# One weight tile on a second DMA queue in the opening of a SwiGLU kernel, with one warm-up matmul fewer

## Chip, cores and metric

The kernel runs on one core of one Trainium2 chip. The metric is the device time of one execution in microseconds (us). Engines are named PE (matmul), PEld (weight load, overlaps PE), ACT (ScalarE), DVE (VectorE), POOL (GpSimd) and SP (SyncE). SP and ACT can both issue DMAs; the notes below call these "SP's queue" and "ACT's queue". The profile's span is about 1.8 us shorter than the measured time, and all times inside a profile count from the span's start.

## The reference

All values are bf16; x is 1 x 2048 x 512, w_gate and w_up are 512 x 1376, w_down is 1376 x 512.

```python
def reference(x, w_gate, w_up, w_down):
    g = silu(x @ w_gate)
    u = x @ w_up
    return (g * u) @ w_down
```

## The kernel before

x is loaded in four chunks of 512 rows, each transposed by the DMA on its way, so that the contracted dimension (512, four blocks `dk` of 128) lies on the partitions. Weights come in growing column blocks. Until the first x chunk and the first gate tile have landed, PE multiplies a constant ("dummies"), so that it is not idle and its clock is let up to full rate.

```python
N_WARM = 11
...
        o = load_x("sp", 0)                      # 512 rows x 512 columns, 512 KB, transposed
        for dk in range(KD):
            got_x[0, dk] = o
        for a, b in ((0, 1), (1, 2), (2, 4), (4, 7), (7, NFT)):
            g = load_w("sp", w_gate, 0, a * P, min(b * P, F))
            u = load_w("sp", w_up, UPH, a * P, min(b * P, F - 32))
            for ft in range(a, b):
                for dk in range(KD):
                    got_g[ft, dk], got_u[ft, dk] = g, u
        ...
        op("act", lambda e: e.activation(adummy[:, 0:4], zero_c, ACT.Silu), inc=False)

        for i in range(N_WARM):
            op("pe", lambda e: e.matmul(banks[7][:, :], lhsT=ones_w, rhs=ones_m, start=True, stop=True), inc=False)
        ...
        def mm_g(n, c, ft, dk):
            deps = [got_x[c, dk], got_g[ft, dk]]
            ...
```

The first real matmul therefore waits for two loads: the whole first x chunk (one transposing DMA) and the first gate tile (128 KB). Everything after it, four chunks of gate and up matmuls with silu on ACT and the product on DVE and then the down projection, is one dense stream on PE.

## Time and profile before

| | before |
|---|---|
| time, median of 3 runs (lowest to highest) | 123.04 us (122.6 to 123.08) |
| span of the profiled run | 121.0 us |
| PE busy | 117.1 us, 97% |
| x chunk issued, landed | 0.73, 4.80 us |
| first gate tile issued, landed | 2.18, 5.45 us |
| first real matmul | 5.59 us |

The page of the kernel before says in its first part which engine is busy, and in its fourth part (the chain of work that ended last) that this work is nearly all on PE.

```profile
PE 117.1 (97%) x540; PEld 53.3 (44%) x550; DVE 43.8 (36%) x64; ACT 30.2 (25%) x51; POOL 0.2 (0%) x4
PE 97%; issue 1%; ACT 0%
```

So, without touching the matmuls, only the two ends can be shortened: the opening, and the 2.5 us from the last matmul's end (about 118.6 us) to the end of the span. The timeline of SP in the opening, kernel before (start, duration, then the instruction; "SPq" is the issue of a DMA, not its transfer):

```profile
0.73 1.39 SPq L123 DMA_TRANSPOSE xT_sb<-in_x_dram  x1
2.18 0.57 SPq L131 DMA_DIRECT2D w_sb<-in_w_gate_dram  x1
2.81 0.48 SPq L131 DMA_DIRECT2D w_sb<-in_w_up_dram  x1
```

The DMA view of the first microseconds, kernel before (size and time from issue to landing):

```profile
w_sb<-in_w_gate_dram SPq DMA_DIRECT2D x1, 128.0 KB, 3.3
xT_sb<-in_x_dram SPq DMA_TRANSPOSE x1, 4.1
```

The gate tile waits 1.45 us for its turn to be issued and lands 0.65 us after x. PE and its weight loads in the opening, kernel before (the bracket is the idle time before, and what ended it):

```profile
0.77 4.85 PE L163 MATMUL bank<-const-bfloat16-1.0 128*128 128x512 bf16 x11 [0.77 <-PEq L302]
5.59 10.76 PE L166 MATMUL bank<-xT_sb,w_sb 128*128 128x512 bf16 x47
4.14 0.15 PEld L163 LDWEIGHTS bank<-const-bfloat16-1.0 128*128 128x128 bf16 x1 [0.28 <-issue]
4.57 0.15 PEld L163 LDWEIGHTS bank<-const-bfloat16-1.0 128*128 128x128 bf16 x1 [0.27 <-issue]
5.56 0.14 PEld L166 LDWEIGHTS bank<-xT_sb,w_sb 128*128 128x128 bf16 x2 [0.84 <-DMA xT_sb<-in_x_dram]
```

Weight loads start 0.43 us apart: PE runs at half rate here (later matmuls start 0.216 us apart). The last line blames x for the wait, but x had landed at 4.80 us; the gate tile, at 5.45 us, is the load whose landing lies just before 5.56 us. A wait for several semaphores has one name in the profile, and it is worth checking against the landings.

### The profile page before, as it was taken

To read this page: it belongs to the slowest core of one execution; us is meant where nothing else is said; L and a number is where in the kernel's file an instruction comes from. 1 tells how busy PE (TensorE), PEld (TensorE's weight loads), DVE (VectorE), ACT (ScalarE), POOL (GpSimd) and SP (SyncE) were. 2 spreads that over 40 slices of the span, in tenths; PEclk is the share of its full clock that TensorE was granted. 3 is DMA by queue.
4 is the path that set the end of the run, shared out by engine and by line. 5 is a ranking of instruction groups with operands and counts; after the bars stand their busy time and mean duration, and the time that the engine had idled before them with its cause. 6 is when DMAs were issued, how large, how long until landed. Compare 5 with 4: busy or idle time off the path is not lost.

```text
span 121.0 us, 1373 instructions
## 1 busy us (share of the span) xinstructions
PE 117.1 (97%) x540; PEld 53.3 (44%) x550; DVE 43.8 (36%) x64; ACT 30.2 (25%) x51; POOL 0.2 (0%) x4
## 2 busy tenths in 40 slices
PE   7999999999999999999999999999999999999991
PEld 2244444444444444444444444344444444444470
DVE  0024334444334444334354334467242233224230
ACT  4032333262333272333262333230000000000001
POOL 0000000000000000000000000000000000000000
PEclk9999999999999999999999999999999999999999
DMA  3999999900000000000000000000211211121121
GB/s 72 245 285 372 262 236 239 355 29 0 0 0 0 0 0 5 0 0 3 0 3 0 0 0 0 5 0 0 87 43 43 87 43 46 51 81 43 43 73 57
DMA packets 17990, 8.51 MB, mean 70 GB/s; under 512 B 11360, under 2 KB 17984, under 8 KB 17984
## 3 DMA queue, kind: packets, MB, share of 16 engines
q1 hardware_dynamic: 17840, 8.36, 25.3%
q8 instruction: 4, 0.07, 0.2%
q10 hardware_dynamic: 144, 0.07, 0.2%
q14 instruction: 2, 0.02, 0.0%
HBM read 4.23 MB, written 2.10 MB: 52 GB/s over the span
## 4 chain that ended last, share of the span: by engine, by line
PE 97%; issue 1%; ACT 0%
PE bank L166 60%; PE bank L247 31%; PE bank L163 4%; PE bank L221 2%; ACT o_sb L254 0%
## 5 line engine op out<-in xcount | busy, mean ns | idle before, releaser
L166 PE MATMUL bank<-xT_sb,w_sb 128*128 128x512 bf16 x330 | 72.6, 380 | 0.3
L166 PEld LDWEIGHTS bank<-xT_sb,w_sb 128*128 128x128 bf16 x336 | 32.9, 98 | 40.4 <-DMA xT_sb<-in_x_dram 0.8
L188 DVE TENSOR_TENSOR hT_sb<-sg_sb,bank 128x512 bf16<-128x512 f32 x40 | 27.5, 688 | 45.3 <-PE bank L166 45.2
L247 PE MATMUL bank<-wd_sb,hT_sb 128*128 128x512 bf16 (+3 forms) x183 | 37.9, 366 | 0.3 <-issue 0.2
L185 ACT ACTIVATE sg_sb<-bank 128x512 f32<-128x512 f32 x40 | 23.8, 596 | 44.6 <-PE bank L166 44.6
L247 PEld LDWEIGHTS bank<-wd_sb,hT_sb 128*128 128x128 bf16 (+1 forms) x187 | 18.2, 98 | 20.2 <-issue 0.4
L255 DVE CAST o_sb<-bank 128x512 bf16<-128x512 f32 (+1 forms) x16 | 10.8, 675 | 23.7 <-PE bank L247 23.7
L254 ACT ACTIVATE o_sb<-bank 128x256 bf16<-128x256 f32 x1 | 0.4, 384 | 38.9 <-PE bank L247 38.9
L163 PE MATMUL bank<-const-bfloat16-1.0 128*128 128x512 bf16 x11 | 4.9, 630 | 0.8 <-PEq L302 0.8
L212 DVE TENSOR_TENSOR hT_sb<-sgx_sb,bank 32x512 bf16<-32x512 f32 x4 | 2.8, 693 | 4.9 <-ACT sgy_sb L210 4.9
L209 ACT ACTIVATE sgx_sb<-bank 32x512 f32<-32x512 f32 x4 | 2.4, 588 | 4.5 <-PE bank L166 4.5
L163 PEld LDWEIGHTS bank<-const-bfloat16-1.0 128*128 128x128 bf16 x11 | 1.5, 143 | 3.2 <-issue 3.2
L227 DVE TENSOR_TENSOR hT_sb<-sgy_sb,bank 64x512 bf16<-64x512 f32 x4 | 2.7, 684 | 0.1
L210 ACT ACTIVATE sgy_sb<-bank 64x512 f32<-64x512 f32 x4 | 2.4, 589 | 0.1
L221 PE MATMUL bank<-xT_sb,w_sb 128*64 128x512 bf16 x16 | 1.9, 382 | 0.0
L159 ACT ACT_TABLE_LOAD x1 | 1.3, 1283 | 0.7 <-PEq L302 0.7
L221 PEld LDWEIGHTS bank<-xT_sb,w_sb 128*64 128x64 bf16 x16 | 0.8, 109 | 1.0 <-issue 0.4
L159 ACT ACTIVATE act_dummy<-const-float32-0.0 128x4 f32<-128x4 f32 x1 | 0.2, 205 | 0.0
L302 POOL MEMSET const-bfloat16-1.0<- 128x1 bf16 x1 | 0.1, 101 | 0.0
L302 POOL MEMSET const-uint8-127<- 128x1 uint8 x1 | 0.1, 101 | 0.0
L302 POOL MEMSET const-float32-0.0<- 128x1 f32 x1 | 0.1, 98 | 0.2 <-issue 0.2
L302 POOL MEMSET const-float32-1.0<- 128x1 f32 x1 | 0.1, 98 | 0.0
## 6 DMA issues: line engine op xcount, KB each, us to landing
out_dram<-o_sb SPq DMA_DIRECT2D x15, 128.0 KB, 1.7
wd_sb<-in_w_down_dram SPq DMA_DIRECT2D x1, 1280.0 KB, 6.8
w_sb<-in_w_gate_dram SPq DMA_DIRECT2D x1, 480.0 KB, 6.0
w_sb<-in_w_up_dram SPq DMA_DIRECT2D x1, 448.0 KB, 6.5
w_sb<-in_w_gate_dram SPq DMA_DIRECT2D x1, 384.0 KB, 5.0
w_sb<-in_w_up_dram SPq DMA_DIRECT2D x1, 384.0 KB, 5.5
w_sb<-in_w_gate_dram SPq DMA_DIRECT2D x2, 128.0 KB, 3.1
w_sb<-in_w_up_dram SPq DMA_DIRECT2D x2, 128.0 KB, 3.3
```

Source lines behind the costliest of these rows:

```text
L159: op("act", lambda e: e.activation(adummy[:, 0:4], zero_c, ACT.Silu), inc=False)
L163: op("pe", lambda e: e.matmul(banks[7][:, :], lhsT=ones_w, rhs=ones_m, start=True, stop=True), inc=False)
L166: return op("pe", lambda e: e.matmul(bank[:, :], lhsT=w_sb[:, dk, col0:col0 + P], rhs=xT_sb[:, dk, c * SC:(c + 1) * SC], start=(dk == 0), ...
L185: s = op("act", lambda e: e.activation(sg_sb[n % NSG][:, :], psG[n % NG][:, :], ACT.Silu), [g, mults[n - NSG] if n >= NSG else None])
L188: mults.append(op("dve", lambda e: e.tensor_tensor(hT_sb[:, ft, c * SC:(c + 1) * SC], sg_sb[n % NSG][:, :], psU[n % NU][:, :], ALU.mult), ...
L209: op("act", lambda e, c=c: e.activation(sgx_sb[c][96:128, :], psX[64:96, :], ACT.Silu), [xm], inc=False)
L210: rest_a[c] = op("act", lambda e, c=c, y0=y0, y1=y1: e.activation(sgy_sb[c][y0:y1, :], psX[0:64, :], ACT.Silu), [xm])
L212: rest_x[c] = op("dve", lambda e, c=c: e.tensor_tensor(hT_sb[64:96, NFF, c * SC:(c + 1) * SC], sgx_sb[c][96:128, :], psX[96:128, :], ALU.m ...
L221: ym = op("pe", lambda e, pi=pi, dk=dk, c=c, y0=y0, y1=y1: e.matmul(psY[pi][y0:y1, :], lhsT=w_sb[:, dk, YC0:YC0 + 64], rhs=xT_sb[:, dk, c ...
L227: rest_y[c] = op("dve", lambda e, pi=pi, c=c, y0=y0, y1=y1: e.tensor_tensor(hT_sb[0:64, NFF, c * SC:(c + 1) * SC], sgy_sb[c][y0:y1, :], ps ...
L247: om = op("pe", lambda e, K=K, fk=fk: e.matmul(bank[:, 0:ncol], lhsT=hT_sb[0:K, fk, t * P:(t + 1) * P], rhs=wd_sb[0:K, fk, c0:c0 + ncol], ...
L255: return op("dve", lambda e: e.tensor_copy(ob[:, a:b], bank[:, a - c0:b - c0]), deps)
```

## The change

The intent: load the first gate tile from ACT's queue, beside the long issue of the x transpose, so that it no longer waits its turn on SP; with x alone left to wait for, one dummy fewer fits.

```diff
-N_WARM = 11
+N_WARM = 10
...
-        HF = 0
         o = load_x("sp", 0)
...
-            g = load_w("sp", w_gate, 0, a * P, min(b * P, F))
+            g = load_w("act" if a == 0 else "sp", w_gate, 0, a * P, min(b * P, F))
```

(`HF` was not used.)

## The prediction

> **What bounds the kernel now.** TensorE. On the page of the kernel before, PE is busy 117.1 us of a span of 121.0 us; the chain of work that ended last is PE for 97%. After the first real matmul no load or eviction holds PE up, so only a shorter opening can help here.
>
> **The opening, from the timeline and the landing times of the loads.** The eleven dummies start at 0.77 us, 0.427 us apart, so the slot after the eleventh is at about 5.42 us. SP issues the x transpose at 0.73 us for 1.39 us; it lands at 4.80 us. The first gate tile is issued at 2.18 us and lands at 5.45 us, the first up tile at 5.90 us. The first real matmul starts at 5.59 us, 0.14 us after the gate tile: that tile ended the wait (the waits view names x, 0.8 us, before that weight load). The first two real matmuls are still slow; from 6.26 us on, starts are 0.216 us apart, so full rate came at about 6.1 us.
>
> **What the change does.** The gate tile is issued from ACT at about 0.73 us, beside the transpose issue. The issue should take about 0.55 us and pushes the 1.28 us activation table load back; the first real activation is at 6.9 us, so this costs nothing. The gate's 128 KB can be moved before the first x packet (2.1 us). Every later SP issue comes about 0.6 us earlier; the up tile takes the gate's old place and should land near 5.4 us, needed at about 6.4 us. Then x alone releases PE: 4.80 + 0.14 = 4.94 us. Ten dummies end at 0.77 + 10 x 0.427 = about 5.0 us. The first real matmul moves from 5.59 to about 5.0 us: 0.59 us.
>
> **How much reaches the end.** Not all. The Trainium skill, "TensorE: Matmul & The Clock Gate", Part 1, says a free-running activity window, not a count of matmuls, sets the release to full rate; this trace agrees in the two spacings, 0.427 and 0.216 us. PE is busy either way, so the release stays near 6.1 us and the 0.59 us are won at half rate: worth about 0.3 us. In runs where it comes before 5.0 us, all 0.59 us are won. Mean about 0.35 us, 0.3%. Later weight tiles land 0.6 us or more ahead of use and move earlier too.
>
> **Prediction: 122.55 us, 122.0 to 123.05 in 8 of 10.** Faster by over 2%: 0.01; within 2%: 0.98; slower by over 2%: 0.01.
>
> **What would show each step right or wrong.**
> - DMA issues: the gate issue on ACT starts near 0.73 us and lands well before 4 us; x lands at 4.7 to 5.0 us.
> - Timeline: first real matmul at 4.95 to 5.1 us, three real matmuls at slow spacing instead of two; full rate from about 6.1 us.
> - Waits: PE waits at most 0.2 us for x, and for no later weights.
> - Span about 120.7 us.
>
> **What would make it wrong.** The Trainium skill, "Perfetto Trace Analysis", section "DMA Instruction — HWDGE", says the descriptor generator is shared and locked. No trace here shows two queues issuing at once. If ACT gets it first, the transpose is delayed by up to about 0.5 us, x lands near 5.3 us and PE waits after the tenth dummy: the gain falls to about 0.1 us. If ACT must wait, gate packets interleave with x's and delay x as much. A gap in PE could also put the full-rate release off by a window: up to 1.5 us slower. The spread of runs before (122.6 to 123.08 us) is as large as the expected gain.

## The result, and the profile after

| | before | after |
|---|---|---|
| time, median of 4 runs | 122.9 us (122.6 to 123.08) | 122.22 us (122.13 to 122.28) |
| span of the profiled run | 121.0 us | 120.4 us |
| gate tile issued, landed | 2.18 (SP), 5.45 us | 0.74 (ACT), 3.14 us |
| x chunk issued, landed | 0.73, 4.80 us | 0.73, 5.14 us |
| first real matmul | 5.59 us | 5.18 us |
| full rate reached | 6.1 us | about 3.5 us |

The ratio was 0.9947, 95% interval 0.9923 to 0.9971: within 2%. A ratio here is the mean time of one kernel's fast runs over that of the other's fast runs of the same rounds, so not quite the ratio of the medians quoted.

The issues in the opening, kernel after, from the timelines of SP and ACT:

```profile
0.73 1.41 SPq L123 DMA_TRANSPOSE xT_sb<-in_x_dram  x1
0.74 0.42 ACTq L131 DMA_DIRECT2D w_sb<-in_w_gate_dram  x1
1.19 1.28 ACT L158 ACT_TABLE_LOAD   x1 [1.19 <-PEq L301]
```

The two issues run side by side, and the transpose's is not lengthened: 1.41 us beside ACT's, 1.39 us alone. The same loads in the DMA view, kernel after:

```profile
w_sb<-in_w_gate_dram ACTq DMA_DIRECT2D x1, 128.0 KB, 2.4
xT_sb<-in_x_dram SPq DMA_TRANSPOSE x1, 4.4
```

The gate tile is early now, but x takes 0.3 us longer to land. PE and PEld in the opening, kernel after:

```profile
0.77 3.65 PE L162 MATMUL bank<-const-bfloat16-1.0 128*128 128x512 bf16 x10 [0.77 <-PEq L301]
5.18 2.12 PE L165 MATMUL bank<-xT_sb,w_sb 128*128 128x512 bf16 x9 [0.77 <-DMA xT_sb<-in_x_dram]
2.86 0.15 PEld L162 LDWEIGHTS bank<-const-bfloat16-1.0 128*128 128x128 bf16 x1 [0.28 <-issue]
3.28 0.15 PEld L162 LDWEIGHTS bank<-const-bfloat16-1.0 128*128 128x128 bf16 x1 [0.28 <-issue]
3.60 0.32 PEld L162 LDWEIGHTS bank<-const-bfloat16-1.0 128*128 128x128 bf16 x2 [0.16 <-issue]
```

Two things are to be seen. PE now truly waits for x, 0.77 us, because its dummies ran out early. And they ran out early because full rate came between 3.28 and 3.60 us: the step between two loads falls from 0.43 to 0.32 us and then two of them fit in 0.32 us. In the kernel before, the dummies ran at half rate to their end. Up to that moment PE did exactly the same in both kernels, so this difference needs another reason than the change. The two spans differ by 0.65 us, of which 0.40 us is the earlier first real matmul (5.59 to 5.18 us) and about 0.25 us is the two matmuls that before still ran at half rate.

So there are two questions. Does the moment of full rate belong to the change or to chance? And why does x land later, so that the start moved by 0.40 us and not by the 0.59 us of the prediction?

### The profile page after: what moved, and what is told of

It reads as the page before. It is cut to its first block, busy times and chain, and to the rows that moved or that the text cites. A ratio compares the mean times of both kernels' runs of the same rounds, so it can differ in the third digit from the quotient of the medians.

```text
span 120.4 us, 1381 instructions
## 1 busy us (share of the span) xinstructions
PE 116.4 (97%) x549; PEld 53.0 (44%) x549; DVE 43.8 (36%) x64; ACT 30.2 (25%) x51; POOL 0.2 (0%) x4
## 4 chain that ended last, share of the span: by engine, by line
PE 94%; DMA 4%; ACT 0%; issue 0%
PE bank L165 60%; PE bank L246 32%; DMA xT_sb<-in_x_dram 4%; PE bank L220 2%; ACT o_sb L253 0%
## 5 line engine op out<-in xcount | busy, mean ns | idle before, releaser
L162 PE MATMUL bank<-const-bfloat16-1.0 128*128 128x512 bf16 x10 | 3.6, 538 | 0.8 <-PEq L301 0.8
```

## The experiments

Twelve kernels ran, all with correct results. Each comparison with before uses runs of before on the same chip, in rounds.

**Theory.** (1) The moment of release to full rate is chance, in a range of about one window (the free-running window of the clock that the prediction names). (2) x lands later because the gate tile's packets use the same DMA engines just before and while x's first packets want to leave. **Rivals.** The release belongs to the kernel; the dummy that was dropped won the time; the later x is noise; the later x is a fixed cost of a second queue that issues at the same moment, whatever its bytes.

### Each kernel again, and each half of the change alone

The kernel before against itself (no edit):

> The kernel before, once more, against itself: ratio 1.000 within 0.3%. It tells what repeats. Theory: the x transpose lands at 4.8 us and the gate tile at 5.4 to 5.5 us in every trace, first real matmul near 5.6 us. Rival, the landing times are noise: x lands anywhere from 4.7 to 5.2 us, as in the kernel after. The moment of the release to full rate (6.1 us in the first trace of before, 3.4 us in that of after) should fall anywhere between about 3 and 6.5 us if it is a free-running window; if it belongs to the kernel, it comes at 6.1 us again.

The changed kernel again (no edit):

> The changed kernel once more. Ratio to before 0.993 to 0.998. Theory: x lands at 5.1 us again (0.34 us later than alone), gate at about 3.1 us, first real matmul near 5.2 us; the start alone is worth 0.40 us (0.3%), and the rest of the 0.65 us between the two first traces was the chance of the release, 0.25 us. If the release belongs to the kernel it comes at 3.4 us again; if it is free-running it may come anywhere from 3 to 6.5 us, and when after 5.2 us it costs half of the difference.

The gate tile on ACT, eleven dummies:

```diff
-N_WARM = 10
+N_WARM = 11
```

> The gate tile on ACT alone, eleven dummies kept. Theory: x lands at 5.1 us. Where the release comes early, the eleven dummies end before that and the start is the same 5.2 us as with ten; where it comes late they end at 5.42 us and the first real matmul is at 5.42 us, but at the slow rate a dummy more costs little. So ratio to before 0.995 to 0.999, at most 0.2% slower than with ten. Rival, dropping the dummy is what won the time: ratio 1.000.

Ten dummies, the gate tile on SP:

```diff
-N_WARM = 11
+N_WARM = 10
```

> Ten dummies alone, the gate tile kept on SP. Theory: the gate tile at 5.45 us holds the first real matmul at 5.6 us as before, ratio 1.000 within 0.2%; only the idle time before it grows (by up to 0.43 us). Rival, the dummy's time was won: ratio 0.996.

| kernel | median us | ratio to before (95%) | x landed | gate landed | first real matmul | full rate from |
|---|---|---|---|---|---|---|
| before again | 122.94 | 1.0017 (0.9998 to 1.0036) | 4.82 | 5.47 | 5.61 | 6.74 |
| after again | 122.54 | 0.9987 (0.9971 to 1.0003) | 5.32 | 3.33 | 5.37 | 5.92 |
| gate on ACT, 11 dummies | 122.36 | 0.9987 (0.9968 to 1.0007) | 5.32 | 3.32 | 5.38 | 5.35 |
| gate on SP, 10 dummies | 122.53 | 0.9992 (0.9979 to 1.0005) | 4.77 | 5.23 | 5.36 | 5.90 |

The median of before in these rounds was 122.64 us. What follows:

- The release does not belong to a kernel. The same kernel before had it at 6.11 and at 6.74 us, the same kernel after at 3.5 and at 5.92 us.
- The 0.65 us of the first comparison did not repeat: here the change is worth 0.0013 x 122.6 = about 0.16 us, and its interval reaches past 1. The two intervals just touch, at 0.9971. The same program against itself came out at 1.0017, so 0.2% is about what such a comparison can be off by. The expectation for the repeat (0.993 to 0.998) was missed.
- The later x is not noise: 4.77 to 4.82 us in three traces with the gate on SP, 5.14 to 5.32 us in three with the gate on ACT.
- The dummy decides little. With eleven, the ratio is the same as with ten. With ten and the gate on SP, the trace shows a first real matmul at 5.36 us, earlier than the 5.6 us that was expected, since in this trace the gate tile landed at 5.23 us; why it was 0.2 us earlier than in the two traces of before is open. The eleventh dummy would have ended at about 5.42 us and so cost it 0.06 us at the most. The time (0.9992) cannot be told from no change.

PE of the changed kernel again, to set beside the first trace of it:

```profile
0.77 4.42 PE L162 MATMUL bank<-const-bfloat16-1.0 128*128 128x512 bf16 x10 [0.77 <-PEq L301]
5.37 1.94 PE L165 MATMUL bank<-xT_sb,w_sb 128*128 128x512 bf16 x7 [0.17 <-DMA xT_sb<-in_x_dram]
```

The ten dummies took 3.65 us in one execution and 4.42 us in the other, with the same program.

### More or fewer bytes beside the transpose

Only a quarter of the gate tile (32 KB) on ACT, the rest behind x on SP:

```diff
-            g = load_w("act" if a == 0 else "sp", w_gate, 0, a * P, min(b * P, F))
+            g = load_w("sp", w_gate, 0, a * P, min(b * P, F), 1 if a == 0 else 0, KD)
+            g0 = load_w("act", w_gate, 0, 0, P, 0, 1) if a == 0 else g
...
-                    got_g[ft, dk], got_u[ft, dk] = g, u
+                    got_g[ft, dk], got_u[ft, dk] = (g0 if dk == 0 else g), u
```

> Only the first quarter of the gate tile (32 KB, the first 128 rows) on ACT; the other 96 KB follow x on SP. The x transpose has landed at 4.77 to 4.82 us alone and at 5.14 to 5.32 us beside the gate tile on ACT. Theory, bytes: x's packets share the DMA engines with the gate's, so a quarter of the bytes delays it by a quarter, x at 4.85 to 4.95 us. Rival, a fixed cost of a second queue that issues beside the transpose: x at 5.1 to 5.3 us again. The rest of the gate lands at about 5.3 us, so the second real matmul waits and the time is that of before within 0.3%.

The first up tile on ACT too (256 KB):

```diff
-            u = load_w("sp", w_up, UPH, a * P, min(b * P, F - 32))
+            u = load_w("act" if a == 0 else "sp", w_up, UPH, a * P, min(b * P, F - 32))
```

> The first up tile on ACT too, so twice the bytes (256 KB) beside the transpose. Theory, bytes: x is delayed by twice as much, to 5.6 to 5.9 us, and the first real matmul to 5.7 to 6.0 us: slower than the changed kernel by 0.3 to 0.5 us, slower than before by 0.1 to 0.3%. Rival, a fixed cost: x at 5.1 to 5.3 us and the time of the changed kernel. Rival, a cost per issue: looks like bytes here, and is told apart by the quarter tile.

Half of the gate tile (64 KB) on ACT, which ran last, as the version that the other runs pointed to:

```diff
-            g = load_w("act" if a == 0 else "sp", w_gate, 0, a * P, min(b * P, F))
+            g = load_w("sp", w_gate, 0, a * P, min(b * P, F), 2 if a == 0 else 0, KD)
+            g0 = load_w("act", w_gate, 0, 0, P, 0, 2) if a == 0 else g
...
-                    got_g[ft, dk], got_u[ft, dk] = g, u
+                    got_g[ft, dk], got_u[ft, dk] = (g0 if dk < 2 else g), u
```

> The version that the runs point to: half of the first gate tile (64 KB) on ACT, the other half behind x on SP, ten dummies. x has landed at 4.77-4.82 us with no gate beside it, at 4.88 with a quarter, at 5.14-5.42 with the whole and at 6.09 with gate and up tile. Theory, bytes: x at 4.95 to 5.1 us, the other half of the gate at about 5.2 us, in time for the third real matmul; first real matmul at 5.0 to 5.15 us instead of about 5.3. With the moments of release seen so far that is worth some 0.1 us over the changed kernel and 0.3 us over before: ratio to before 0.9965 to 0.9985. Rival, the quarter's early x was chance: x at 5.1 to 5.4 us and the ratio of the changed kernel.

| on ACT beside the transpose | x's 500th packet leaves | x landed | first real matmul | median us | ratio to before (95%) |
|---|---|---|---|---|---|
| nothing (before, before again, 10 dummies) | 2.69 to 2.76 us | 4.77 to 4.82 us | 5.36 to 5.61 us | | |
| 32 KB | 2.68 us | 4.88 us | 4.99 us | 122.58 | 0.9984 (0.9964 to 1.0003) |
| 64 KB | 2.73 us | 4.76 us | 4.98 us | 122.28 | 0.9968 (0.9954 to 0.9981) |
| 128 KB (four traces) | 3.05 to 3.26 us | 5.14 to 5.42 us | 5.18 to 5.47 us | 122.54 | 0.9987 (0.9971 to 1.0003) |
| 256 KB | 3.03 us | 6.09 us | 6.13 us | 122.91 | 1.0016 (0.9991 to 1.0042) |

(The 128 KB row has the changed kernel's time from its second comparison; the first gave 122.22 us and 0.9947. Its four traces are the two of the changed kernel, the one with eleven dummies and the late try below that was not late.) The DMA view of the first microseconds with gate and up tile on ACT, then with half of the gate tile:

```profile
w_sb<-in_w_gate_dram ACTq DMA_DIRECT2D x1, 128.0 KB, 2.4
w_sb<-in_w_up_dram ACTq DMA_DIRECT2D x1, 128.0 KB, 4.6
xT_sb<-in_x_dram SPq DMA_TRANSPOSE x1, 5.4
```

```profile
w_sb<-in_w_gate_dram ACTq DMA_DIRECT2D x1, 64.0 KB, 2.1
w_sb<-in_w_gate_dram SPq DMA_DIRECT2D x1, 64.0 KB, 2.8
xT_sb<-in_x_dram SPq DMA_TRANSPOSE x1, 4.0
```

The fixed cost of a second queue is out: with 32 and 64 KB on ACT the transpose takes 4.1 and 4.0 us to land, as in the kernel before, and with 256 KB 5.4 us. But the delay is not in proportion either; half the tile cost nothing (x at 4.76 us, expected 4.95 to 5.1 us) and the two tiles cost more than twice the one (6.09 us, expected 5.6 to 5.9 us), so the theory, as the expectations put it, missed both. The packets in the trace show more. The DMA view of the first 2.5 us counts them by queue (q1 is SP's, q10 ACT's; packets, MB, share of the 16 engines), for the kernel before, the changed kernel and the one with half of the tile on ACT:

```profile
q1 hardware_dynamic: 293, 0.08, 12.7%
```

```profile
q10 hardware_dynamic: 436, 0.11, 22.7%
q1 hardware_dynamic: 4, 0.00, 0.2%
```

```profile
q10 hardware_dynamic: 272, 0.07, 12.6%
q1 hardware_dynamic: 242, 0.06, 10.8%
```

By 2.5 us the changed kernel has sent 4 of x's packets instead of 293; with half of the tile it is 242. ACT's first packets leave at 1.75 to 1.90 us, and x's first, with nothing on ACT, at 2.11 to 2.13 us. The quarter had sent 135 of its 144 packets by the time x's first left (2.12 us), the half 180 of 272 (x's first at 2.19 us, ACT's last at 2.42 us), and x's 500th packet leaves when it does without them. That the half's last 92 packets, which left among x's first, cost nothing is measured; why is not shown. The whole tile has its last packet at 2.80 to 3.08 us, x's first is put off to 2.36 to 2.46 us, and x's 500th leaves 0.3 to 0.6 us later than without it. The gate and up tiles then keep sending during most of x's stream. This agrees with what the Trainium skill says in "DMA: Bandwidth & Descriptors", section "Issuing engines are not separate DMA queues": DMAs from different engines run on the same 16 DMA engines and interleave, and a second issuer saves only the time of issue.

The half tile is the best version found: 0.9968, its whole interval below 1, on the chip of the first group. PE of it in the opening:

```profile
0.77 4.42 PE L163 MATMUL bank<-const-bfloat16-1.0 128*128 128x512 bf16 x10 [0.77 <-PEq L302]
4.98 2.27 PE L166 MATMUL bank<-xT_sb,w_sb 128*128 128x512 bf16 x7
```

The first real matmul follows the dummies without a gap, and the second half of the gate tile, landed at 5.00 us from SP, is in time for the third. Whether it beats the changed kernel in time is not settled: the two were not compared in the same rounds, 0.9968 lies between the changed kernel's two ratios, and only the first-matmul times (4.98 against 5.18 to 5.47 us) tell them apart.

### The same bytes later

The gate tile on ACT, but behind the activation table load and the dummy activation:

```diff
+        op("act", lambda e: e.activation(adummy[:, 0:4], zero_c, ACT.Silu), inc=False)
         got_x = {}
...
-        op("act", lambda e: e.activation(adummy[:, 0:4], zero_c, ACT.Silu), inc=False)
```

> The gate tile stays on ACT but is issued after the activation table load and the dummy activation, at about 2.2 us instead of 0.73 us, so it loses its head start before x's first packet. Theory, bytes shared packet by packet: x lands at 5.2 to 5.5 us, as late as beside an early gate or later, gate at 4.7 to 5.2 us, first real matmul 5.3 to 5.5 us. Rival, the delay comes from the two issues at the same moment: x at 4.8 us again and the gate at 5.0 to 5.2 us, first real matmul at 5.2 us.

This try failed as an experiment. From the timeline of ACT in that kernel:

```profile
0.73 1.28 ACT L135 ACT_TABLE_LOAD   x1 [0.73 <-PEq L300]
0.80 0.43 ACTq L131 DMA_DIRECT2D w_sb<-in_w_gate_dram  x1
```

The DMA was issued at 0.80 us, while the table load ran: ACT's sequencer, which issues DMAs, did not wait for its engine here. It counts as one more trace of the changed kernel's opening (x at 5.42 us, first real matmul at 5.47 us, median 122.51 us, ratio 0.9988, 0.9967 to 1.001). It was made really late by a wait for the third dummy:

```diff
         for i in range(N_WARM):
-            op("pe", lambda e: e.matmul(banks[7][:, :], ...), inc=False)
+            d = op("pe", lambda e: e.matmul(banks[7][:, :], ...), inc=(i == 2))
+            if i == 2:
+                got_g[0, 0].deps.append(d)
```

> The late gate again, now really late: the load on ACT waits for the third dummy, so it is issued at about 2.3 us, just after the transpose's issue ends at 2.13 us (the try after the table load was issued at 0.80 us all the same, because ACT's sequencer ran ahead of its engine). Theory, bytes shared packet by packet: the gate's packets meet x's in mid-flow and x lands at 5.2 to 5.5 us, gate at 4.7 to 5.3 us, first real matmual 5.3 to 5.55 us: no better than before by more than 0.2%. Rival, what delays x is the issue at the same moment, which shifts x's first packet from 2.12 to 2.36-2.45 us: first packet at 2.12 us and x at 4.8 to 4.9 us again.

The gate was issued at 2.24 us, x's first packet left at 2.13 us and x landed at 4.97 us, so x lost at most 0.2 us; the gate's first packet left only at 4.18 us, when x's stream was nearly through, and it landed at 5.69 us, later than from SP. The first real matmul came at 5.82 us, the median was 122.93 us, ratio 1.0003 (0.9978 to 1.0028). Both expectations missed the gate's landing, and x's landing, taken alone, is nearer to the rival (a delay from two issues at the same moment: 4.8 to 4.9 us) than to the theory (5.2 to 5.5 us). That rival is out because of the quarter and the half, which were issued at the same moment as the transpose and put x off by 0.1 us at most. That a queue which starts first delays x, while one that starts behind x is itself held back, fits "the same engines"; the rule by which packets of the two queues take turns is not packet by packet in these traces, and it stays open. One of the four runs, at 124.99 us, counts as slow (over 1.5% above the fastest run of its kernel) and is left out of the ratio; no trace of it exists.

### Tries to have x sooner

The first x chunk as four transposes of 128 columns, six dummies:

```diff
-        o = load_x("sp", 0)
         for dk in range(KD):
-            got_x[0, dk] = o
+            got_x[0, dk] = load_x("sp", 0, dk)
...
-N_WARM = 10
+N_WARM = 6
```

> A try to beat both: the first x chunk is transposed in four loads of 128 columns, so that the first real matmul needs a quarter of x, and the dummies are cut to six (end 3.33 us). If a quarter transpose is issued in about 0.5 us and lands at about 3.3 us, with 0.6 us between quarters, the first real matmul is at about 3.4 us and the first four run at half rate as the quarters land; the gate group is then done about 1 us earlier than in the changed kernel and the time falls by up to 0.5 us where the release comes late, or stays where it comes early. If each quarter costs the 1.4 us issue of the whole, the last lands near 8 us and the kernel is over 1 us slower.

As two halves of 256 rows (`NX = 2`), or four quarters of 128 rows (`NX = 4`), nine dummies (the first matmul waits for all parts; those lines are left out):

```diff
-        o = load_x("sp", 0)
+        xp = [dma("sp", lambda e, i=i: e.dma_start_transpose(
+            xT_sb[:, :, i * SC // NX:(i + 1) * SC // NX], xf[i * SC // NX:(i + 1) * SC // NX, :])) for i in range(NX)]
...
-N_WARM = 10
+N_WARM = 9
```

> A try to beat both: the first x chunk is transposed as two halves of 256 rows, the gate tile on ACT, nine dummies (end 4.6 us). Splitting by columns cost 1.25 us of issue for each quarter, against 1.39 us for the whole, so the issue seems to go by rows. If so, a half is issued in about 0.7 us, x's first packet leaves at about 1.5 us instead of 2.1, and with 640 KB to move at the rate seen (512 KB in 2.68 us) all has landed at about 4.7 to 5.0 us: first real matmul 4.8 to 5.1 us, 0.2 to 0.4% faster than before on average. If the issue costs about 1.2 us whatever the rows, the second half is issued at 3.2 us and lands at 5.3 us or later: no gain.

> As the two halves, in four quarters of 128 rows. If the issue goes by rows with little fixed cost (0.4 us a quarter), x's first packet leaves at about 1.2 us and all has landed by 4.4 to 4.8 us, the first real matmul at 4.6 to 4.9 us. If each has a fixed cost of 0.5 us or more beside it, the fourth is issued at about 3.5 us and lands at 5 us or later, slower than the two halves.

All three lost or gained nothing: 127.09 us (1.0355, 1.0317 to 1.0393), 122.9 us (1.0046, 0.9973 to 1.0119) and 126.55 us (1.0306, 1.0257 to 1.0356). The timelines of SP say a part of why, in this order for columns, two row halves and four row quarters:

```profile
0.73 5.13 SPq L124 DMA_TRANSPOSE xT_sb<-in_x_dram  x4
```

```profile
0.73 2.66 SPq L139 DMA_TRANSPOSE xT_sb<-in_x_dram  x2
```

```profile
0.73 5.22 SPq L139 DMA_TRANSPOSE xT_sb<-in_x_dram  x4
```

Each part costs about 1.3 us of issue, like the whole chunk (1.39 us), whichever way it is cut. The last part landed at 7.34, 5.82 and 7.32 us. The row quarters show a second loss. PE in their opening, and then the windows view (stretch, length, PE busy and count, the other engines, granted clock, DMA share, GB/s):

```profile
0.77 3.86 PE L164 MATMUL bank<-const-bfloat16-1.0 128*128 128x512 bf16 x9 [0.77 <-PEq L303]
7.36 1.94 PE L167 MATMUL bank<-xT_sb,w_sb 128*128 128x512 bf16 x5 [2.73 <-DMA xT_sb<-in_x_dram]
8.20:11.20 3.00, 3.00 (x8) 0.99 (x7) 0.50 (x1) 0.60 (x1) 0.00 (x0) 0.50 1.04 262
11.20:14.00 2.80, 2.80 (x14) 1.27 (x13) 0.87 (x2) 1.02 (x2) 0.00 (x0) 1.00 0.99 314
```

After the idle 2.73 us the clock fell back to 0.50: by the trace's clock record from 7.78 to 11.19 us, and in the first line of the view above eight matmuls ran in a time that takes fourteen at full rate. The columns fell back too, and for longer, from 6.93 to 13.76 us, though no idle gap of PE there was over 0.93 us; in the 3.4 us before, PE was busy for only 1.17 us. PE at half rate loses half of the time that it works so: by estimate 1.7 us of the row quarters' 3.2 us and 2.6 us of the columns' 4.4 us (differences of the traced spans to before). So in both more than half of the loss is the clock and not the issue. One of four runs of the two halves (idle 1.24 us) was at 124.51 us, 1.6 us over its others; a fallback of 3.41 us would cost 1.7 us and is a likely reason, but no trace of that run exists.

### One formula for all the traces

In every trace that had no fallback, the span is

span = first real matmul + 115.20 us + half of the stretch, if any, between the first real matmul and the release.

115.20 us is what followed the first real matmul in the trace of the changed kernel, where the release came before it. Release times are read from the trace's clock record, in two kernels from the spacing of the dummies. The record shows the window too: every stretch between two changes of the clock in it is a multiple of 3.413 us (3.413, 6.827, 112.64 and 116.05 us), and the releases, 3.5 to 6.7 us, spread over just less than one such step. So the clock changes on a fixed step, and where the step lies against the kernel's start differs from execution to execution.

| kernel | first real matmul | release | span by formula | span measured |
|---|---|---|---|---|
| before | 5.59 | 6.11 | 121.05 | 121.03 |
| before again | 5.61 | 6.74 | 121.37 | 121.35 |
| gate on SP, 10 dummies | 5.36 | 5.90 | 120.83 | 120.80 |
| after | 5.18 | 3.5 | 120.39 | 120.39 |
| after again | 5.37 | 5.92 | 120.84 | 120.81 |
| gate on ACT, 11 dummies | 5.38 | 5.35 | 120.58 | 120.57 |
| quarter of the gate on ACT | 4.99 | 6.59 | 120.99 | 120.99 |
| half of the gate on ACT | 4.98 | 6.18 | 120.78 | 120.79 |
| gate and up on ACT | 6.13 | 4.49 | 121.33 | 121.34 |
| gate on ACT, late | 5.82 | 4.64 | 121.02 | 121.01 |

The formula holds to 0.03 us. (Two traces without a fallback are not in the table and fit as well: the gate tile after the table load, 120.67 us against 120.67, and the two halves, 121.07 against 121.08, if their release came before the first real matmul, as the even spacing from there on shows.) It says that an earlier start is worth its full size only where the release comes before it, and half where the release comes later, and that the release alone, anywhere from 3.5 to 6.7 us, moves the time of one and the same kernel by up to (6.74 - 5.61) / 2 = 0.56 us. That is as large as the whole effect of the change. With the release times of these ten traces put into the formula, a start moved from 5.6 to 5.35 us is worth about 0.2 us on average, and one moved to 5.0 us about 0.4 us; these are estimates. The second comparison of the changed kernel (0.16 us) and that of the half tile (0.0032 x 122.7 = 0.39 us) lie near them; the first comparison of the changed kernel (0.65 us) lies above. That its four runs had mostly early releases is argued from the formula and the one trace, not shown for the other three runs.

## Why the prediction was right or wrong, point by point

- **Time and class: right, in part by luck.** 122.22 us (and 122.54 us in the second comparison) against 122.55 us, within the range, within 2%. The range of 1.05 us was three times the gain that was expected (0.35 us), so the hit says little about the steps. About 0.25 us of the first result came from the early release, which is chance.
- **The gate tile ended the wait before, not x: right.** x had landed at 4.80 us, and with the gate away from SP it is x that PE waits for.
- **The gate issue on ACT at 0.73 us, landed well before 4 us, activation table load pushed back at no cost: right** (0.74, 3.14 us; table load at 1.19 us, first real activation at 6.26 us).
- **The fear of a locked descriptor generator: not shown.** The Trainium skill, "Perfetto Trace Analysis", section "DMA Instruction — HWDGE", describes a generator that is locked for one user at a time; here both issues ran from 0.73 us on, and the transpose's took 1.41 us instead of 1.39 us.
- **x lands at 4.7 to 5.0 us, as if the gate tile passed for nothing: wrong.** The step "the gate's 128 KB can be moved before the first x packet" failed. The gate's first packet left at 1.82 us and its last at 2.80 us, x's first at 2.46 us instead of 2.12 us; x landed at 5.14 us, and at 5.32 us in the repeat. The prediction knew this cost, but tied it to the case that ACT must wait.
- **Every later SP issue about 0.6 us earlier, the up tile landed near 5.4 us: wrong.** The up tile was issued 0.6 us earlier (2.20 us), but its issue took 0.91 us instead of 0.48 us, and it landed at 5.75 us (before: 5.90 us); the issues after it came only 0.17 to 0.19 us earlier. It cost nothing, since PE needed it later.
- **First real matmul at 5.0 us, 0.59 us earlier: too large by a third or more.** It was 0.40 us in the first pair of traces, 0.24 us in the second.
- **Full rate stays near 6.1 us, so the gain counts half: right in kind, wrong as a fixed time.** The half is what the formula shows. But 6.1 us was one draw: thirteen traces with a reading range from 3.5 to 6.7 us. The prediction said so in words ("a free-running window") and then used one value. Of the three slow real matmuls that it expected, the first trace after had none.
- **PE waits at most 0.2 us for x: wrong in the first trace (0.77 us), right in the second (0.17 us).** The same cause: early full rate ends the dummies early.
- **Span about 120.7 us: 120.4 us, and 120.8 us in the repeat.** Two misses of the sum had opposite signs in the first trace: the later x took 0.2 us away from the gain in the start, and the early release gave at least as much back.

## What to carry to other kernels

A second queue saves the wait for a turn to issue, not engine time: put on it few bytes, most of which can leave before the first queue's own packets do, and measure how many are free (here 64 KB cost x nothing, 128 KB cost it 0.3 to 0.6 us, 256 KB 1.3 us). Before an effect of a few tenths of a microsecond in the opening is believed, split each trace's span into the first real work and the moment of full rate, because the second is chance and can be as large as the effect. An issue with a fixed cost, as the transpose's 1.3 us, is not shortened by cutting the transfer into parts on the same queue. And when a try leaves PE waiting in the opening, look at the clock before the wait is blamed: in two of the tries here the fallback cost more, by estimate, than the later start.

## What the Trainium skill lacked or had wrong

- "TensorE: Matmul & The Clock Gate", Part 1, was right that the release is tied to a free-running window of about 3.4 us: the clock changed in steps of 3.413 us. Its spread of plus or minus 500 ns for the moment of release is too small: thirteen traces put it between 3.5 and 6.7 us with PE busy from 0.77 us on. It says that the count of slow matmuls varies from run to run; it lacks what this does to comparisons: by the formula up to 0.56 us between executions of one kernel of 123 us, as large as the effect of the change.
- The same page's advice, in "Why this matters for your kernels", is to have no PE idle gaps over about 3 us. That is not enough: 2.73 us of idle PE were followed by 3.4 us at a granted clock of 0.50, and in the columns' trace gaps of at most 0.93 us, with PE busy for 1.17 of 3.4 us, by 6.8 us at 0.50.
- "DMA: Bandwidth & Descriptors", section "Issuing engines are not separate DMA queues", says that the transfers interleave, and not in what order. Another section of that page, "Queues, rings and completion order", has each engine turn between its queues a packet at a time, of up to 64 descriptors; no run here tests the size of such a turn. They show that the lead matters: the queue that started 0.3 us ahead had 397 of its 528 packets out before x's first (2.46 instead of 2.12 us), and the gate tile issued at 2.24 us, behind x, sent its first packet at 4.18 us, after 1970 of SP's.
- No page read here gives the issue time of a DMA transpose on this chip by size: 1.3 us for 128 KB and 256 KB parts, 1.39 us for the 512 KB chunk.
- No page read here says that the granted clock in the profile's windows view reads 1.00 before the first release, while the matmuls start 0.427 us apart, at half rate.
